# Attention with a threshold and a squared-ReLU FFN on one core: weight norms from TensorE products, low words to integers on GpSimd, other prices in the planner

## The chip, the cores and the metric

One Trainium2 chip, one core of it. The metric is the device time of one execution in microseconds (us), given as the median of several runs. Beside it stands one execution taken with the hardware profiler, from which all durations inside the kernel come. The five engines of the core run their own instruction lists in fixed order: TensorE (PE, with its weight loads listed as PEld), VectorE (DVE), ScalarE (ACT), GpSimd (POOL) and SyncE (SP), which here issues all transfers.

## The reference

Eight batches, eight heads, 576 positions, 64 columns per head. Scores under the row maximum by more than tau are dropped; the result goes through an FFN with 512 columns in and out and 2048 in the middle.

```python
scores = scale * np.matmul(q, k.transpose(0, 1, 3, 2))
thresh = np.max(scores, axis=-1, keepdims=True) - tau
scores = np.where(scores >= thresh, scores, -1000000000.0)
attn = np.exp(scores - np.max(scores, axis=-1, keepdims=True))
attn = attn / (np.sum(attn, axis=-1, keepdims=True) + 1e-09)
x = np.matmul(attn, v)            # heads side by side: 4608 x 512
h = x @ w_in                      # 512 x 2048
r = np.maximum(h, 0.0)
out = (s * (r * r) + b) @ w_out   # 2048 x 512
```

The two weight matrices come as 64-bit floats. The core sees each number as two 32-bit words, the low one first.

## The kernel before

**Attention.** A tile is 128 queries of one head against 576 keys. Batch 0 (the "plain" tiles, 36 of them) is worked in 32-bit floats, because it runs while the weights aren't ready: scores on TensorE (L457), row maximum on VectorE (L460), threshold on GpSimd (L462), exponential on ScalarE (L464), mask and row sum on VectorE (L466), sum on GpSimd (L469), reciprocal on VectorE (L471), normalising on GpSimd (L472), five transposes on TensorE (L480), copy out on ScalarE (L484), product with V on TensorE (L493) and its copy on ScalarE (L497). The tiles of the other seven batches work with pairs of 16-bit pieces (L514 to L532), and with_v multiplies two heads' finished tiles by V (L547), one group of 28 products for 256 or 320 columns.

**FFN.** A block is 256 rows. For each of 16 slices f of the middle dimension a step makes 12 products with the pieces of w_in (L756), ReLU, square and split (L760 to L765), and 6 products with the pieces of w_out (L771). L685 sums the rows of w_out for the constant b.

**Weights.** A slice f of w_in and one of w_out, 128 x 512 numbers each, are loaded by load_weights (L567, L570) from the SyncE queue, 512 KB apiece. In weights, ScalarE turns the high word so that it becomes, once shifted by three bits, the upper part of a 32-bit float (L589); VectorE shifts it (L592); ScalarE squares the high word alone (L594, L603), TensorE sums the squares of w_in over rows with a matrix of ones (L599), VectorE takes the maximum (L601), and the squares of w_out are summed by ScalarE itself. pieces_of_weights joins the low word's three highest bits to it (whole, L645). When all 32 norms are there, weight_scales finds powers of two for the two matrices (L610 to L627). Only with these can ScalarE and VectorE make the 16-bit pieces (L653, L658) that the FFN's products need.

**Order.** Every operation is given to a planner (class Plan) with its engine, the time that it occupies the engine, the time to its result, what it reads and writes, and a due time in tiles. The planner places all operations by these prices, forward and backward several times, and keeps the order with the earliest end. Operations of GpSimd, and those of VectorE that are marked dve2, exclude each other in the planner. The result is a fixed order for each engine. Prices thus don't only describe the work, they decide the order of everything. On SyncE the weight loads stand in one queue with the loads of q, k and v, later with the moves of attention pieces (L370, L537) and the stores.

At the start, 76 products on zeros (L901) keep TensorE occupied while nothing else is there.

Of the kernel before, what the change touches and what calls it, by code (L numbers as in the profile page):

```python
# [9 lines left out]
F32 = mybir.dt.float32  # L10
F32R = mybir.dt.float32r
F16, BF16 = mybir.dt.float16, mybir.dt.bfloat16
I32 = mybir.dt.int32
# [127 lines left out]
def tile_attention_ffn(ctx: ExitStack, tc: tile.TileContext, qT, kT, v, tau, w_in, w_out, s, b, out):  # L141


    nc = tc.nc
# [38 lines left out]
    wmost, wnorm, wpower, wback = const("wmost", [P, 2, NF]), const("wnorm", [P, 4]), const("wpower", [P, 4, 2]), const("wback", [P, 2])  # L183
    ones16, onesb = const("ones16", [P, P], F16), const("onesb", [P, P], BF16)
# [355 lines left out]
    def with_v(g, at):  # L540
# [8 lines left out]
        cost = len(slots) * (0.42 * g.n + 8) + 300  # L549
# [11 lines left out]
    def load_weights(f, at):  # L561
# [8 lines left out]
        plan.add("SP", (1800, 6700), lambda: nc.sync.dma_start(out=raw(1).rearrange("p f t -> p (f t)"),  # L570
                                           in_=w_out[f * P:(f + 1) * P, :]), [], [(f"w{f}", "o")], at)

    def weights(f, at):
# [6 lines left out]
        tag = f"t{f % 2}"  # L580

# [3 lines left out]
        def squares():  # L585
            return early("eb")[:, 2 * DM * (f % 2):2 * DM * (f % 2) + DM // 2].bitcast(BF16)
        for u, k in (0, "i"), (1, "o"):
            kr = f"w{f}", k
            act((563, 667), lambda u=u: nc.scalar.activation(  # L589
                out=words(1, u).bitcast(F32), in_=words(1, u).bitcast(F32), func=AF.Prelu, scale=2.0 ** -112, alpha=-2.0 ** 32),  # L590
                [kr], [kr], at)
            dve2((328, 418), lambda u=u: nc.vector.tensor_scalar(  # L592
                out=words(1, u), in0=words(1, u), scalar1=3, scalar2=None, op0=ALU.logical_shift_left), [kr], [kr], at)
        act((563, 667), lambda: nc.scalar.activation(out=squares(), in_=words(1, 0).bitcast(F32), func=AF.Square),  # L594
            [(f"w{f}", "i")], [tag], at)

        def sizes():
            for c in range(NC):
                nc.tensor.matmul(bank["h"][:, 0:P], onesb, squares()[:, c * P:(c + 1) * P], start=(c == 0), stop=(c == NC - 1))  # L599
        pe(NC, P, sizes, [tag, "ones16"], ["h"], at)  # L600
        dve((200, 290), lambda: nc.vector.tensor_reduce(  # L601
            out=wmost[:, 0, f:f + 1], in_=bank["h"][:, 0:P], axis=mybir.AxisListType.X, op=ALU.max), ["h"], [("wmost", 0, f)], at)
        act((640, 860), lambda: nc.scalar.activation(  # L603
            out=early("eb")[:, 2 * DM * (f % 2) + DM // 2:2 * DM * (f % 2) + DM].bitcast(BF16), in_=words(1, 1).bitcast(F32),
            func=AF.Square, accum_out=wmost[:, 1, f:f + 1]), [(f"w{f}", "o")], [("wmost", 1, f), (tag, 1)], at)

    def weight_scales(at):

        most = [("wmost", u, f) for u in range(2) for f in range(NF)]
        dve((90, 170), lambda: nc.vector.tensor_reduce(  # L610
            out=wnorm[:, 0:2], in_=wmost, axis=mybir.AxisListType.X, op=ALU.max), most, ["wnorm"], at)
        dve((90, 170), lambda: nc.vector.tensor_reduce(
            out=wnorm[:, 2:3], in_=wmost[:, 1], axis=mybir.AxisListType.X, op=ALU.add), most, [("wnorm", 2)], at)
        top = bank["pv"][:, 384:386]
        pe(1, 64, lambda: nc.tensor.matmul(top, ones.bitcast(F32), wnorm[:, 2:4], start=True, stop=True),
           ["ones", "wnorm", ("wnorm", 2)], [("top", 384)], at)
        dve((72, 155), lambda: nc.vector.tensor_scalar(
            out=wpower[:, 0, 0:1], in0=wnorm[:, 0:1], scalar1=LEAST, scalar2=None, op0=ALU.max), ["wnorm"], ["wpower"], at)
        dve((72, 155), lambda: nc.vector.tensor_scalar(
            out=wpower[:, 0, 1:2], in0=top[:, 0:1], scalar1=LEAST, scalar2=None, op0=ALU.max), [("top", 384)], ["wpower"], at)  # L620
# [19 lines left out]
    def pieces_of_weights(f, at):  # L640

        def whole(u):
            raw = lazy["raw", f, u]
# [382 lines left out]
```

## Time and profile before

| | us |
|---|---|
| median of 3 runs | 1164.04 (1164.00 to 1165.47) |
| profiled execution, its own time | 1164.36 |
| profiled execution, span from the first to the last instruction | 1162.6 |
| TensorE busy | 1126.4 |
| ScalarE busy | 930.3 |
| VectorE busy | 858.7 |
| GpSimd busy | 779.2 |
| mean granted TensorE clock | 0.997 of full |

Busy times count an instruction from its first to its last moment. Neighbouring instructions of one engine overlap by a little, so what an instruction takes of its engine is the distance to the next one, or the piece that the chain of waits gives it, and it is shorter than the shown duration. Matmul ends are modelled. The idle time "before" a group is put down to what released it last.

### The profile page before, as it was taken

What the parts mean: (1) busy time and instruction counts of PE and PEld (TensorE: products, weight loads), DVE (VectorE), ACT (ScalarE), POOL (GpSimd) and SP (SyncE); (2) the same over time, 40 slices, a digit from 0 to 9 for tenths busy, and PEclk for the clock granted to TensorE, in tenths of its full rate; (3) what the DMA queues carried; (4) which work ended last, traced back from release to release, by engine and by line L of the source; (5) the groups of instructions that cost most, each with busy time, mean ns of one, the idle gap of its engine ahead of it and who ended that gap; (6) DMA issues with size and microseconds to landing.
All of it is one profiled execution on the core that took longest, in us unless ns stands there. A gap on an engine that the chain in (4) does not pass through costs nothing.

```text
span 1162.6 us, 26056 instructions
## 1 busy us (share of the span) xinstructions
PE 1126.4 (97%) x8778; PEld 820.4 (71%) x8778; DVE 858.7 (74%) x1840; ACT 930.3 (80%) x2159; POOL 779.2 (67%) x1327
## 2 busy tenths in 40 slices
PE   8888999989999999999999999999999999999998
PEld 7666766657777777766777777777777777766665
DVE  7998898897887888897778877788787878730011
ACT  4999898878889898987888888878888889754443
POOL 4568688777877787776667777778777878532200
PEclk9999999989999999999999999999999999999999
DMA  7930278998799788987778878887878779800000
GB/s 246 392 106 22 52 140 166 177 182 174 149 173 178 156 160 173 165 169 141 156 136 161 152 154 151 163 151 149 173 155 166 138 146 185 123 19 1 19 19 19
DMA packets 361334, 164.52 MB, mean 142 GB/s; under 512 B 315120, under 2 KB 336112, under 8 KB 361200
## 3 DMA queue, kind: packets, MB, share of 16 engines
q1 hardware_dynamic: 361200, 162.86, 68.7%
q8 instruction: 69, 1.13, 0.4%
q14 instruction: 65, 0.53, 0.1%
HBM read 62.52 MB, written 9.44 MB: 62 GB/s over the span
## 4 chain that ended last, share of the span: by engine, by line
PE 78%; ACT 7%; DVE 5%; DMA 5%; issue 2%; POOL 2%; SPq 2%; DVEq 0%; ACTq 0%; POOLq 0%
PE h L756 29%; PE o L771 29%; PE pv L547 8%; PE s L514 5%; PE t L514 5%; DMA iw<-in_moe_w_in_dram 2%; DMA eb<-en 1%; ACT en L529 1%; ACT em L521 1%; DVE st L517 1%; DVE en L532 1%; DVE em L523 1%; ACT em L464 1%; DVE iw L785 1%; ACT iw L760 1%
## 5 line engine op out<-in xcount | busy, mean ns | idle before, releaser
L756 PE MATMUL h<-xp,iw 128*128 128x256 f16 x3456 | 427.1, 273 | 7.3 <-ACT iw L760 5.5
L756 PEld LDWEIGHTS <-iw 128*128 128x128 f16 x3456 | 330.1, 98 | 91.5 <-issue 11.3
L771 PE MATMUL o<-ow,gh 128*128 128x512 f16 x1080 | 322.9, 381 | 1.0 <-DVE iw L785 1.0
L765 POOL TENSOR_TENSOR gl<-iw,gh 128x256 f16<-128x256 f32 x272 | 199.8, 735 | 125.1 <-ACT gh L764 95.8
L532 DVE SCALAR_TENSOR_TENSOR en<-em,st,en 128x576 f16<-128x576 f32 x252 | 237.2, 947 | 23.8 <-ACT en L529 22.8
L529 ACT ACTIVATE en<-em,st 128x576 f16<-128x576 f32 x252 | 192.9, 771 | 19.3 <-DVE st L528 14.7
L771 PE MATMUL o<-ow,gl 128*128 128x512 f16 x540 | 204.8, 379 | 0.0
L760 ACT ACTIVATE iw<-h 128x256 f32<-128x256 f32 x288 | 109.6, 380 | 118.9 <-PE h L756 112.3
L771 PEld LDWEIGHTS <-gh 128*128 128x128 f16 x1152 | 100.3, 98 | 78.0 <-issue 5.1
L519 POOL TENSOR_SCALAR st<-st,bound 128x1 f32<-128x1 f32 x252 | 108.4, 431 | 52.4 <-DVE st L517 27.7
L763 ACT ACTIVATE iw<-iw 128x256 f32<-128x256 f32 x288 | 120.0, 417 | 3.8
L764 ACT CAST gh<-iw 128x256 f16<-128x256 f32 x288 | 116.1, 404 | 5.4 <-PE o L771 1.0
L523 DVE SCALAR_TENSOR_TENSOR em<-s,st,em 128x576 f32<-128x576 f32 x126 | 102.3, 812 | 19.8 <-ACT em L521 10.4
L517 DVE TENSOR_REDUCE st<-t 128x1 f32<-128x576 f32 x126 | 94.9, 753 | 29.1 <-PE t L514 28.5
L526 POOL TENSOR_SCALAR st<-st 128x1 f32<-128x1 f32 x252 | 80.2, 318 | 53.1 <-DVE em L523 20.5
L523 DVE SCALAR_TENSOR_TENSOR em<-t,st,em 128x576 f32<-128x576 f32 x126 | 102.3, 812 | 18.1 <-ACT em L521 10.6
L517 DVE TENSOR_REDUCE st<-s 128x1 f32<-128x576 f32 x126 | 94.8, 753 | 27.7 <-PE s L514 26.2
L521 ACT ACTIVATE em<-t,st 128x576 f32<-128x576 f32 x126 | 92.7, 735 | 21.2 <-DVE st L517 16.0
L547 PE MATMUL pv<-ea,v 128*64 128x256 f16 (+1 forms) x784 | 107.9, 289 | 0.0
L547 PE MATMUL pv<-eb,v 128*64 128x256 f16 (+1 forms) x784 | 106.9, 288 | 0.5 <-DMA eb<-en 0.4
L521 ACT ACTIVATE em<-s,st 128x576 f32<-128x576 f32 x126 | 92.7, 736 | 16.0 <-DVE st L517 15.7
L771 PEld LDWEIGHTS <-gl 128*128 128x128 f16 x576 | 56.3, 98 | 67.9
(190 smaller groups left out, 1864.0 us busy)
## 6 DMA issues: line engine op xcount, KB each, us to landing
rk<-in_k_dram SPq DMA_DIRECT2D x57, 288.0 KB, 4.2
rq<-in_q_dram SPq DMA_DIRECT2D x56, 288.0 KB, 4.1
ow<-k SPq DMA_DIRECT2D x56, 216.0 KB, 2.9
iw<-in_moe_w_in_dram SPq DMA_DIRECT2D x16, 512.0 KB, 7.3
ow<-in_moe_w_out_dram SPq DMA_DIRECT2D x16, 512.0 KB, 7.9
out_dram<-iw SPq DMA_DIRECT2D x32, 256.0 KB, 3.0
rv<-in_v_dram SPq DMA_DIRECT2D x56, 128.0 KB, 2.8
kt<-k SPq DMA_DIRECT2D x56, 72.0 KB, 2.6
```

The source lines that it names most:

```text
L514: nc.tensor.matmul(ps[:, hf], stat, kk(hf), start=(n == 0), stop=(n == len(seq) - 1))
L517: dve((667, 750), lambda: nc.vector.tensor_reduce(out=top, in_=ps, axis=mybir.AxisListType.XY, op=ALU.max, negate=True), [bk], [(ks_, 0)], ...
L521: act((636, 740), lambda: nc.scalar.activation(out=halves, in_=ps, func=AF.Exp, bias=top, scale=1.0), [bk, (ks_, 0)], [em_k], i - 0.5)
L523: dve((740, 900), lambda: nc.vector.scalar_tensor_tensor(out=halves, in0=ps, scalar=line, in1=halves, op0=ALU.is_ge, op1=ALU.mult, accum_o ...
L529: act((668, 774), lambda: nc.scalar.activation(out=pieces[:, 0:S], in_=ex, func=AF.Copy, scale=unit), [em_k, (ks_, 3)], [en_k], i)
L532: dve2((740, 825), lambda: nc.vector.scalar_tensor_tensor(out=pieces[:, S + T:2 * S + T], in0=ex, scalar=unit, in1=pieces[:, 0:S], op0=ALU ...
L547: nc.tensor.matmul(ps[j * D:(j + 1) * D], hd.v[:, (n + 1) % 5, u * D:(u + 1) * D], lazy[("ea", "eb")[j]][:, n, g.c0:g.c0 + g.n], start=(i ...
L756: nc.tensor.matmul(ps, wi[w][f][:, c * P:(c + 1) * P], x[:, u, c, :], start=(c == 0 and i == 0), stop=(c == NC - 1 and i == 2))
L760: act((357, 473), lambda: nc.scalar.activation(out=g(), in_=ps, func=AF.Relu, scale=H_DOWN), [h, (f"w{(0, 1, 5)[k3]}", "i", 2)], [kg], at)
L763: act((320, 417), lambda: nc.scalar.activation(out=g(), in_=g(), func=AF.Square), [kg], [kg], at)
L765: do((712, 735) if not self.last else (340, 425), lambda: eng.tensor_tensor(out=lo, in0=g(), in1=hi, op=ALU.subtract), [kg, f"gh{k3}"], [f ...
L771: nc.tensor.matmul(bank["o"][:, t, :], a[:, ts_], w, start=(f == 0 and i == 0), stop=(f == NF - 1 and i == 2))
```

## The change

- **Squares and shifts go.** L592, L594, L599, L601 and L603 with their scratch space are removed. ScalarE's only work per weight piece before the scales is L589.
- **Low words on GpSimd.** A new instruction per piece (32 in all) reads the upper 16 bits of each low word as an unsigned 16-bit integer (one of four half words, a step of 8 bytes), multiplies by 2^-13 and subtracts just under one half, and writes the result as a 32-bit integer over the low word: its three highest bits.
- **The join shifts.** whole now shifts the high word left by three and joins the new integer, in one VectorE instruction as before. It stands in weights, ahead of the norms, and has to wait for GpSimd.
- **Norms from products.** A new function weight_sizes, once for four slices, reads the upper halves of the joined floats as 16-bit floats (bf16, every second half word) and lets TensorE multiply each 128 x 128 part with itself: 16 products for w_in into four stretches of 128 columns of a PSUM bank, VectorE's maximum over 512 columns, then 16 for w_out into 128 columns, and the maximum over these. No ones matrix in bf16 is made any more.
- **Scales.** weight_scales takes the maximum over four values for each matrix, turns the two columns through TensorE, takes the maximum over 128, multiplies by a 2 x 2 identity and spreads the two numbers over all partitions with one product. Before it had two reductions and one product.
- **Prices.** A group with V costs 14 (0.417 n + 3) + 150 ns in the plan for 14 (0.42 n + 8) + 300, and a weight load 1320 ns of the queue and 5200 ns to landing for 1800 and 6700.

```diff
-        cost = len(slots) * (0.42 * g.n + 8) + 300
+        cost = len(slots) * (0.417 * g.n + 3) + 150
...
-        plan.add("SP", (1800, 6700), lambda: nc.sync.dma_start(out=raw(0).rearrange("p (c f) t -> p c (f t)", c=NC),
+        plan.add("SP", (1320, 5200), lambda: nc.sync.dma_start(out=raw(0).rearrange("p (c f) t -> p c (f t)", c=NC),
...
+        def whole(u):
+            raw = lazy["raw", f, u]
+            lazy["whole", f, u] = raw.rearrange("p f t -> p (f t)")[:, 0:DM].bitcast(F32)
+            nc.vector.scalar_tensor_tensor(out=lazy["whole", f, u].bitcast(I32), in0=raw[:, :, 1], scalar=3, in1=raw[:, :, 0],
+                                           op0=ALU.logical_shift_left, op1=ALU.bitwise_or)
...
-            dve2((328, 418), lambda u=u: nc.vector.tensor_scalar(
-                out=words(1, u), in0=words(1, u), scalar1=3, scalar2=None, op0=ALU.logical_shift_left), [kr], [kr], at)
-        act((563, 667), lambda: nc.scalar.activation(out=squares(), in_=words(1, 0).bitcast(F32), func=AF.Square),
-            [(f"w{f}", "i")], [tag], at)
...
-        act((640, 860), lambda: nc.scalar.activation(
-            out=early("eb")[:, 2 * DM * (f % 2) + DM // 2:2 * DM * (f % 2) + DM].bitcast(BF16), in_=words(1, 1).bitcast(F32),
-            func=AF.Square, accum_out=wmost[:, 1, f:f + 1]), [(f"w{f}", "o")], [("wmost", 1, f), (tag, 1)], at)
+            pool((700, 720), lambda u=u: nc.gpsimd.tensor_scalar(
+                out=words(0, u), in0=lazy["raw", f, u].bitcast(U16)[:, :, 1], scalar1=2.0 ** -13, scalar2=2.0 ** -14 - 0.5,
+                op0=ALU.mult, op1=ALU.add), [kr], [kr + (0,)], at)
+            dve2((602, 685), lambda u=u: whole(u), [kr, kr + (0,)], [kr], at)
+
+    def weight_sizes(k, at):
+        fs, d = range(4 * k, 4 * k + 4), [slice(c * P, (c + 1) * P) for c in range(NC)]
+
+        def top(f, u):
+            return lazy["whole", f, u].bitcast(BF16).rearrange("p (f t) -> p f t", t=2)[:, :, 1]
+
+        def grams(u):
+            for n, f in enumerate(fs):
+                for c in range(NC):
+                    nc.tensor.matmul(bank["h"][:, d[0 if u else n]], top(f, u)[:, d[c]], top(f, u)[:, d[c]],
+                                     start=(c == 0 and not (u and n)), stop=(c == NC - 1 and (not u or n == 3)))
+        for u, key, w in (0, "i", 4 * P), (1, "o", P):
+            pe(4 * NC, P, lambda u=u: grams(u), [(f"w{f}", key) for f in fs], ["h"], at)
+            dve((100 + 1.06 * w, 190 + 1.06 * w), lambda u=u, w=w: nc.vector.tensor_reduce(
+                out=wmost[:, u, k:k + 1], in_=bank["h"][:, 0:w], axis=mybir.AxisListType.X, op=ALU.max), ["h"], [("wmost", u, k)], at)
...
+        turned, top = bank["h"][0:2, 0:P], bank["pv"][:, 384:386]
+        pe(1, 4 * P, lambda: nc.tensor.matmul(turned, wnorm[:, 0:2], ident(), start=True, stop=True), ["ident", "wnorm"], ["h"], at)
+        dve((210, 290), lambda: nc.vector.tensor_reduce(
+            out=wnorm[0:2, 2:3], in_=turned, axis=mybir.AxisListType.X, op=ALU.max), ["h"], [("wnorm", 2)], at)
...
-            dve2((602, 685), lambda u=u: whole(u), [kr], [kr], at)
...
+        if f % 4 == 3:
+            events.append((WEIGHTS_EACH * f + 0.1, lambda f=f: weight_sizes(f // 4, 2.5 + WEIGHTS_EACH * f)))
```

More of the change, by code (lines that the diff above doesn't have):

```diff
@@ L12 @@
 F16, BF16 = mybir.dt.float16, mybir.dt.bfloat16
-I32 = mybir.dt.int32
+I32, U16 = mybir.dt.int32, mybir.dt.uint16
 AF = mybir.ActivationFunctionType
@@ L182, in tile_attention_ffn @@
     power = [const(f"power{i}", [P, 5, 4]) for i in range(2)]
-    wmost, wnorm, wpower, wback = const("wmost", [P, 2, NF]), const("wnorm", [P, 4]), const("wpower", [P, 4, 2]), const("wback", [P, 2])
-    ones16, onesb = const("ones16", [P, P], F16), const("onesb", [P, P], BF16)
+    wmost, wnorm, wpower, wback = const("wmost", [P, 2, 4]), const("wnorm", [P, 4]), const("wpower", [P, 4, 2]), const("wback", [P, 2])
+    wtop = const("wtop", [P, 2])
+    ones16 = const("ones16", [P, P], F16)
     vs = [const(f"vs{i}", [P, 4]) for i in range(2)]
@@ L607, in weight_scales @@
     def weight_scales(at):
-        most = [("wmost", u, f) for u in range(2) for f in range(NF)]
+        most = [("wmost", u, k) for u in range(2) for k in range(4)]
         dve((90, 170), lambda: nc.vector.tensor_reduce(
             out=wnorm[:, 0:2], in_=wmost, axis=mybir.AxisListType.X, op=ALU.max), most, ["wnorm"], at)
-        dve((90, 170), lambda: nc.vector.tensor_reduce(
-            out=wnorm[:, 2:3], in_=wmost[:, 1], axis=mybir.AxisListType.X, op=ALU.add), most, [("wnorm", 2)], at)
@@ L617, in weight_scales @@
         dve((72, 155), lambda: nc.vector.tensor_scalar(
-            out=wpower[:, 0, 0:1], in0=wnorm[:, 0:1], scalar1=LEAST, scalar2=None, op0=ALU.max), ["wnorm"], ["wpower"], at)
+            out=wtop[0:2], in0=ident()[0:2, 0:2], scalar1=wnorm[0:2, 2:3], scalar2=None, op0=ALU.mult), [("wnorm", 2), "ident"], ["wtop"], at)
+        pe(1, 64, lambda: nc.tensor.matmul(top, ones.bitcast(F32), wtop, start=True, stop=True), ["ones", "wtop"], [("top", 384)], at)
         dve((72, 155), lambda: nc.vector.tensor_scalar(
-            out=wpower[:, 0, 1:2], in0=top[:, 0:1], scalar1=LEAST, scalar2=None, op0=ALU.max), [("top", 384)], ["wpower"], at)
+            out=wpower[:, 0], in0=top, scalar1=LEAST, scalar2=None, op0=ALU.max), [("top", 384)], ["wpower"], at)
@@ L640, in pieces_of_weights @@
     def pieces_of_weights(f, at):
-        def whole(u):
-            raw = lazy["raw", f, u]
-            lazy["whole", f, u] = raw.rearrange("p f t -> p (f t)")[:, 0:DM].bitcast(F32)
-            nc.vector.scalar_tensor_tensor(out=lazy["whole", f, u].bitcast(I32), in0=raw[:, :, 0], scalar=29, in1=raw[:, :, 1],
-                                           op0=ALU.logical_shift_right, op1=ALU.bitwise_or)
         def high(u):
@@ L894, in zeros @@
         nc.gpsimd.memset(ones16, 1.0)
-        nc.gpsimd.memset(onesb, 1.0)
     pool((700, 700), zeros, [], ["ones", "qt0", "qt1", "ones16"], -10)
@@ L911, in bounds @@
     def bounds():
-        for t in [vm.bitcast(F32), wnorm] + norm:
+        for t in [vm.bitcast(F32), wtop] + norm:
             nc.gpsimd.memset(t, 0.0)
-    pool((900, 900), bounds, [], ["vm", "norm0", "norm1", "wnorm", ("wnorm", 2)], -8)
+    pool((900, 900), bounds, [], ["vm", "norm0", "norm1", "wtop"], -8)
     def margins():
```

14 lines of the change are left out of this document (1 added, 13 removed).

## The prediction

> **What bounds the kernel now.** I read the page first, then stretches of the early part, then groups and the chain in the stretch that the change touches. TensorE looks saturated in the mean:
>
> ```profile
> span 1162.6 us, 26056 instructions
> PE 1126.4 (97%) x8778; PEld 820.4 (71%) x8778; DVE 858.7 (74%) x1840; ACT 930.3 (80%) x2159; POOL 779.2 (67%) x1327
> ```
>
> The mean hides two stages. The windows (columns: window, its length, then the busy time of each engine with its count, granted clock, DMA share, GB/s) part them:
>
> ```profile
> 30.00:60.00 30.00, 25.65 (x226) 20.41 (x225) 29.39 (x73) 29.55 (x61) 16.41 (x30) 1.00 1.06 394
> 23.00:90.00 67.00, 58.45 (x519) 45.89 (x520) 64.48 (x163) 65.79 (x134) 39.82 (x72) 1.00 0.71 251
> 90.00:98.00 8.00, 6.48 (x47) 4.71 (x45) 7.73 (x20) 5.40 (x13) 7.38 (x12) 1.00 0.00 1
> ```
>
> And two rows with the times of the stage: L589 rewrites weights from 23.1 us on, and the first conversion with the scales, L653, starts at 97.7 us.
>
> ```profile
> L589 ACT ACTIVATE iw<-iw x16: 667/705/777, 23.1 to 83.0; 128x512 f32<-128x512 f32 x16
> ```
> ```profile
> 97.70 1.34 ACT iw L653 x2
> ```
>
> From 23 us to 90 us, within which all squares are taken (the groups below count 16 and 16 of them), ScalarE is busy 65.8 of 67 us and VectorE 64.5: both are full, while TensorE works on tiles of batch 0 only (its busy time includes the modelled tails of matmuls, so it has more air than it shows). The weight scales come out at 97.7 us, and only then can the big products of L756 and L771 start. After that TensorE has more work than it can do: what it waits for from 110 us to the end is small, the largest two being
>
> ```profile
> PE h L756 <- ACT iw L760: 5.0, 7, 1.0
> PE t L514 <- DVE em L523: 4.1, 4, 2.4
> ```
>
> (total us, times, longest). So the end moves with the time at which TensorE gets weights, less what it does of batch 0 meanwhile. The change works exactly on the 23 to 98 us stage, and, by the plan's prices, on the order of everything.
>
> **ScalarE: the squares go.** Groups between 23 and 90 us, then pieces of the chain, which give what one instruction takes of its engine:
>
> ```profile
> L589 ACT ACTIVATE ow<-ow 128x512 f32<-128x512 f32 x16 | 11.5, 719 | 0.0
> L589 ACT ACTIVATE iw<-iw 128x512 f32<-128x512 f32 x16 | 11.4, 712 | 0.0
> L603 ACT ACTIVATE eb<-ow 128x512 bf16<-128x512 f32 x16 | 11.4, 721 | 0.0
> L594 ACT ACTIVATE eb<-iw 128x512 bf16<-128x512 f32 x16 | 11.2, 702 | 0.0
> ```
> ```profile
> 47.68 0.58 ACT eb L594
> 49.45 0.67 ACT eb L603 x2
> ```
>
> 16 x 0.58 + 16 x 0.67 = 20.0 us of ScalarE go. In the stage it falls from 65.8 to about 46 of 67 us: it stops being a bound.
>
> **VectorE: shifts and small maxima go, joins come forward.**
>
> ```profile
> L645 DVE SCALAR_TENSOR_TENSOR iw<-iw 128x512 int32<-128x512 int32 x13 | 8.9, 685 | 0.1
> L645 DVE SCALAR_TENSOR_TENSOR ow<-ow 128x512 int32<-128x512 int32 x13 | 8.9, 682 | 0.0
> L592 DVE TENSOR_SCALAR iw<-iw 128x512 int32<-128x512 int32 x16 | 7.1, 444 | 0.1
> L592 DVE TENSOR_SCALAR ow<-ow 128x512 int32<-128x512 int32 x16 | 6.9, 431 | 0.3 <-ACT ow L589 0.2
> L601 DVE TENSOR_REDUCE wmost<-h 128x1 f32<-128x128 f32 x16 | 4.5, 280 | 0.2
> ```
> ```profile
> 65.75 0.34 DVE iw L592
> 66.21 0.20 DVE wmost L601
> 94.94 0.75 DVE wpower L621
> 95.69 0.60 DVE iw L645
> 96.36 0.59 DVE ow L645
> ...
> 249.55 0.67 DVE st L517
> ```
>
> Removed: 32 x 0.34 + 16 x 0.20 = 14.1 us. Added: four maxima over 512 columns and four over 128. The latter are 0.20 each; the former lie between that 0.20 for 128 columns and the 0.67 that a maximum over 576 columns takes (L517), and I take 0.67: 4 x 0.87 = 3.5 us. Moved: the join (L645 before) must now stand ahead of the products, and 6 of the 32 joins are today done after 90 us; they come into the stage, 6 x 0.60 = 3.6 us. VectorE goes from 64.5 to about 57.5 of 67 us. It too stops being the bound.
>
> **GpSimd: 32 new instructions.** Nothing before shows 16-bit integers turned into 32-bit ones on GpSimd. Nearest is its scaling of 512 floats, L324; the low bound is that row, the high one the mean with waits of L472 in this stage (0.82):
>
> ```profile
> L324 POOL TENSOR_SCALAR k<-k,bound x2: 686/688/691, 15.6 to 80.5; 128x512 f32<-128x512 f32 x2
> L472 POOL TENSOR_SCALAR em<-em,st x36: 737/746/1750, 12.2 to 135.2; 128x576 f32<-128x576 f32 x36
> L462 POOL TENSOR_SCALAR st<-st,bound x36: 260/448/1217, 9.5 to 130.4; 128x1 f32<-128x1 f32 x36
> L469 POOL TENSOR_SCALAR st<-st x36: 190/258/761, 11.2 to 133.7; 128x1 f32<-128x1 f32 x36
> ```
> ```profile
> L472 POOL TENSOR_SCALAR em<-em,st 128x576 f32<-128x576 f32 x21 | 17.1, 817 | 10.6 <-DVE st L471 6.9 <-PE h L599 1.5 <-DVE norm L722 1.4
> L462 POOL TENSOR_SCALAR st<-st,bound 128x1 f32<-128x1 f32 x20 | 10.6, 532 | 8.1 <-DVE st L460 7.9
> L469 POOL TENSOR_SCALAR st<-st 128x1 f32<-128x1 f32 x20 | 5.9, 296 | 8.2 <-DVE em L466 7.3
> ```
>
> (First fence: shortest/median/longest of the whole run in ns.) I take 0.69, so 32 x 0.69 = 22.1 us. Looked at alone GpSimd has room: 39.8 + 22.1 = 62 of 67. But look at how a one-column instruction that takes 0.26 can take 0.62:
>
> ```profile
> 50.83 0.68 DVE L645 SCALAR_TENSOR_TENSOR ow<-ow 128x512 int32<-128x512 int32 x1
> 51.02 0.62 POOL L462 TENSOR_SCALAR st<-st,bound 128x1 f32<-128x1 f32 x1 [0.72 <-DVE st L460]
> ```
>
> It began inside a join and ended 0.13 us after it: the two engines exclude each other while VectorE reads two tensors. So the joins, the shifts and all of GpSimd share one resource. Its demand in the stage before: 21 x 0.74 + 20 x 0.26 + 20 x 0.19 = 24.5, plus GpSimd's other 11 instructions as shown (39.8 - 17.1 - 10.6 - 5.9 = 6.2), plus 26 x 0.60 + 32 x 0.34 = 26.5: 57.2 of 67 us. After: -10.9 for the shifts, +3.6 for the six joins, +22.1: 72.0 of 67. A bound at 98% has been swapped for one at 107%. What eases it is the 0.13 just seen: an instruction of 0.26 had done half of its work under the wait. If half of GpSimd's then 104 instructions win 0.13 each, the demand is 65.2. So the stage ends between 1.8 us sooner and 5 us later; I take **+1.0**, nearer the easy end because the waiting pair is seen in the trace.
>
> The Trainium skill, page SBUF — State Buffer, section "Who interferes with whom", states the rule for this: a VectorE instruction with two SBUF inputs contends with a GpSimd instruction that reads SBUF, and the one that comes second is fully blocked. By that rule taken strictly nothing overlaps and the stage is 5 us longer, not 1; the trace agrees on the blocking (0.62 for 0.26), not on the whole duration. The Trainium skill's page GPSIMD Engine Reference, section "7. Performance pitfalls for Q7 kernels", puts about 1.9 cycles on an element at strides up to 8 bytes, which the new instruction just keeps; at the 1.2 GHz of its section "1. Specifications" an estimate by that page of the skill is 0.81 us in place of 0.69, or 3.8 us more on the shared resource. No row here has a strided GpSimd read.
>
> **TensorE** gets 128 products of 128 columns for 64, some 4 us more over 67 us, in which it waits for batch 0's tiles; they cost nothing while it waits, 4 us if it were full.
>
> **The way from the last weight to the scales.** Today: square, sum, maximum, scales. After: integers (0.69), join (0.60), 16 + 16 products (about 1 us each) with a maximum behind each group, then a turn through TensorE, one more maximum, one more multiplication. Over the shift (0.34) and square (0.67) this is 0.69 + 0.60 + 1.0 + 0.2 - 1.0 = 1.5, and the turn with its maximum, multiplication and hand-overs some 1.8: 3.3 us later. TensorE goes on with tiles meanwhile; I charge half, **+1.6** (bounds 0 and 3.3). Against it, the joins leave the stretch behind 90 us: two lie on the chain itself (95.69 and 96.36 above), 1.2 us, and four more held up VectorE before the first weights; half of their 2.4 counts: **-2.4** together (bounds -3.6 and -1.2).
>
> **Tiles run smoother.** TensorE's waits for ScalarE between 8 and 98 us,
>
> ```profile
> PE pv L493 <- ACT rv L484: 3.1, 3, 1.3
> PE t L480 <- ACT x L484: 2.8, 3, 1.1
> ```
>
> stood behind squares in ScalarE's queue. With 20 us of air a part goes, though each tile now passes a fuller GpSimd three times: **-1.6** (bounds -5.9 and +3).
>
> **The plan's prices.** A group of products with V is priced 14 x (0.42 n + 8) + 300: 1.92 us for 256 columns and 2.29 for 320; the new price gives 1.69 and 2.06. The trace has
>
> ```profile
> 294.29 2.02 PE pv L547 x28
> 311.77 1.65 PE pv L547 x28
> ```
>
> so the new price is right, and 56 groups no longer pretend 15 us of TensorE time. This alters the order on every engine until 1020 us. What a truer order can win is bounded by TensorE's waits there (9.1 us in the two largest rows); it can lose as easily. **-2.0** (bounds -6 and +4). A weight load is priced 1.32 us of the queue for 1.8; 512 KB at the 394 GB/s above is 1.33, so this is right too. Its landing is priced 5.2 us for 6.7, while the page has
>
> ```profile
> iw<-in_moe_w_in_dram SPq DMA_DIRECT2D x16, 512.0 KB, 7.3
> ```
>
> and that is too early by 2.1; the list of waits up to 100 us names no weight load, so it costs nothing as long as the engines run behind the loads, and 2.1 once if they don't.
>
> **The sum**, against the profiled execution (1164.36 us, of which 1162.6 is the span; the median of the runs is 1164.04, 0.3 less): +1.0 + 1.6 - 2.4 - 1.6 - 2.0 = -3.4, so **1161 us**. Its own bounds, with the terms not all at one end: 1154 to 1168.
>
> **Rivals.**
> *VectorE sets the stage.* If the overlap of GpSimd and the joins is larger than seen, the stage shrinks towards VectorE's 57.5 us. Half of the 9.5 us gained reaches the end, since fewer tiles are then done at that time: 1161 - 5 - 3 (the plan's term at its good end) = 1153. For it: VectorE and ScalarE are the engines that show full. Against: the 0.62.
> *The shared port decides* (the slower side). Every join and every GpSimd instruction excludes the other in full: 72.0 for 67, +5.0, with the longer way to the scales in full, +3.3, and only the two joins on the chain saved, -1.2: 1164.4 + 7.1 = 1171. It decides from the point at which the demand passes 67 us: with no overlap, a new instruction of 0.53 us; with half overlapped, one of 0.75. The strict rule of the Trainium skill's page SBUF — State Buffer, cited above, is this rival.
> *The loads are expected too early.* With the landing priced 2.1 us short, ScalarE and VectorE stop in their fixed order on weights between 23 and 60 us, and input loads of batch 0 on the same SyncE queue fall behind weights while DMA is at 1.06 of its share: 2.1 for the first weight, about as much for one late tile: 1168.
> *Nothing moves.* One full resource takes the place of another, and the new order wins nothing: 1164.
>
> **Chances.** Forecast 0.42, of which 0.06 ends within 0.2% (2.3 us, about what a measurement of this kernel can tell from no change); VectorE sets the stage 0.11; nothing moves 0.15; shared port 0.25; early loads 0.07. So faster 0.36 + 0.11 = 0.47, within 0.21, slower 0.32. The range for 8 in 10 reaches to the VectorE case on one side and to the port case on the other: 1152 to 1172; the forecast's own is 1154 to 1168.
>
> **What would show it.** The stage: between the first and the last join, VectorE under 90% and ScalarE near 70% if the shared resource is the bound; GpSimd's new instruction 0.69 alone and stretched beside joins; joins of 0.68 growing to 1 us and more. The first L653 after 97.7 us means the stage didn't shorten; before 93 the VectorE rival. The plan: TensorE's waits behind 110 us. The forecast is wrong if the scales come over 4 us later or earlier than today, or if the difference arises after 150 us.

## The result: 1175.9 us, slower by 0.9%

| | before | after |
|---|---|---|
| median of four runs each, us | 1164.4 (1164.0 to 1165.5) | 1175.9 (1174.7 to 1177.2) |
| profiled execution, us | 1164.36 | 1177.11 |
| its span, us | 1162.6 | 1175.3 |
| mean granted TensorE clock | 0.997 | 0.991 |

The ratio is 1.0088 with a 95% interval [1.0072, 1.0104] (the two medians alone stand as 1.0099). The forecast of 1161 us was wrong, and so was its range up to 1172. The page's first lines after:

```profile
span 1175.3 us, 26160 instructions
PE 1136.5 (97%) x8844; PEld 830.2 (71%) x8844; DVE 853.7 (73%) x1800; ACT 911.7 (78%) x2111; POOL 803.1 (68%) x1358
```

ScalarE gave up 18.6 us, VectorE 5.0, GpSimd took 23.9 more, and TensorE started 66 more products. The windows of the changed kernel (columns as in the prediction):

```profile
23.00:90.00 67.00, 58.17 (x524) 46.17 (x523) 55.72 (x121) 46.15 (x81) 58.88 (x93) 0.97 0.68 224
30.00:45.00 15.00, 10.98 (x92) 8.79 (x92) 10.80 (x23) 9.11 (x16) 13.69 (x20) 0.89 0.93 314
90.00:98.00 8.00, 7.53 (x82) 6.16 (x81) 7.40 (x14) 4.51 (x8) 7.48 (x13) 1.00 0.60 147
180.00:220.00 40.00, 33.58 (x238) 24.06 (x236) 34.26 (x71) 30.16 (x69) 27.30 (x49) 0.91 0.94 180
260.00:280.00 20.00, 14.13 (x94) 9.36 (x91) 17.89 (x38) 13.73 (x28) 14.47 (x26) 0.83 0.96 177
```

TensorE starts 524 products from 23 to 90 us for 519, although 112 of them serve the norms for 64 before: tiles fell back. In the same window ScalarE is at 46.2 us (the prediction had about 46) and VectorE at 55.7 (57.5). GpSimd is busy 58.9 of 67 us, and 13.7 of 15 between 30 and 45 us, a stretch in which every other engine has air. But two later stretches stand out as much: TensorE is busy 33.6 of 40 us at 180 and 14.1 of 20 at 260, at a clock of 0.91 and 0.83. Before, the same stretches read

```profile
180.00:220.00 40.00, 37.47 (x301) 27.21 (x299) 32.52 (x71) 34.77 (x84) 32.96 (x53) 1.00 0.85 165
260.00:280.00 20.00, 20.00 (x166) 14.83 (x166) 15.68 (x37) 17.06 (x43) 14.86 (x23) 0.95 0.88 182
```

**A ledger of TensorE.** Busy time is a poor measure of a pipelined engine. So I count the products in stretches of 8 to 100 us and give each a price, most of them from undisturbed pieces of the chain: 0.1105 us for one of L759 (1.33 for 12), 0.2165 for L774 (0.65 for 3), 0.0655 for L548 (the mean of 1.65 and 2.02 for 28), 0.1235 for L515 (the chain has 0.52 for 4, so 0.13, a little more), 0.2425 for L458 (0.97 for 4), 0.11 for L481 (0.55 for 5), 0.062 for L494, 0.217 for L688, and about 0.06 for a product that serves the norms. What is left of the time is "idle" (waits, products on zeros, and what a halved clock costs). A product that lies across the border of two stretches counts in both, so idle time is understated, and not by the same amount in every run; a difference of 1 or 2 us in it means nothing. Counted once, by its start, the first row of the table is 34.4 and 36.4, the second 18.7 and 27.7, the third 24.3 and 22.5.

| idle, us | before | after |
|---|---|---|
| from 0 to 110 us | 33.1 | 33.7 |
| from 110 to 300 us | 15.5 | 24.6 |
| from 300 to 1100 us | 20.5 | 18.9 |

The span grew by 12.7 us. Some 4 of these are, by count and price, the 64 additional products, and idle time up to 110 us did not shrink to make up for them. Another 9.1 come between 110 and 300 us, long after the changed stage; 1.6 come back later. The prediction had named this as a sign against it: a difference that arises after 150 us.

**What the stage looks like.** Timeline rows of the changed kernel, first VectorE, then GpSimd, then ScalarE (start, us, engine, line; in brackets the idle time before and what ended it):

```profile
31.62 0.70 DVE L587 SCALAR_TENSOR_TENSOR ow<-ow 128x512 int32<-128x512 int32 x1 [0.65 <-POOL ow L595]
32.88 0.69 DVE L587 SCALAR_TENSOR_TENSOR iw<-iw 128x512 int32<-128x512 int32 x1 [0.55 <-POOL iw L595]
...
36.40 0.69 DVE L587 SCALAR_TENSOR_TENSOR iw<-iw 128x512 int32<-128x512 int32 x1 [1.32 <-POOL iw L595]
```
```profile
30.92 0.67 POOL L595 TENSOR_SCALAR ow<-ow 128x512 int32<-128x512 uint16 x1
31.67 1.17 POOL L595 TENSOR_SCALAR iw<-iw 128x512 int32<-128x512 uint16 x1
```
```profile
42.64 0.69 ACT L485 COPY rv<-t 128x640 f32<-128x640 f32 x1 [4.60 <-PE t L481]
```

A new integer instruction (L595) takes 0.64 to 0.67 us alone. The next one begins 0.05 us after a join and lasts 1.17: it ends 0.52 us after the join, so of its 0.65 only 0.13 went on under the join, the very overlap that the prediction read from the 0.62 of L462. The rule of the Trainium skill, page SBUF — State Buffer, section "Who interferes with whom", is that the ports which the two share are an exclusive lock; that is nearly what the trace shows. The next join waits for this integer, and a little later ScalarE waits 4.60 us for transposes: between 30.9 and 37.6 us GpSimd runs five integers among its work for the tiles. Where the chain of waits before was ScalarE's from 43 to 64 us, with squares in it, GpSimd's work stands in it after, from 65 to 74 us:

```profile
65.75 1.19 POOL iw L595
67.02 0.70 POOL st L470
...
68.82 0.72 POOL em L473
...
69.87 0.66 POOL ow L595
```

Between 23 and 90 us the joins wait 6.0 us for integers:

```profile
L587 DVE SCALAR_TENSOR_TENSOR iw<-iw 128x512 int32<-128x512 int32 x16 | 12.7, 797 | 3.3 <-POOL iw L595 3.3
L595 POOL TENSOR_SCALAR iw<-iw 128x512 int32<-128x512 uint16 x16 | 12.3, 771 | 1.3
L595 POOL TENSOR_SCALAR ow<-ow 128x512 int32<-128x512 uint16 x15 | 11.4, 760 | 1.2
...
L587 DVE SCALAR_TENSOR_TENSOR ow<-ow 128x512 int32<-128x512 int32 x14 | 10.4, 743 | 2.7 <-POOL ow L595 2.7
```

The first conversion starts at 107.9 us, 10.2 later than before, the last product for the norms at 96.0:

```profile
L610 PE MATMUL h<-ow x64: 218/218/221, 43.4 to 96.0; 128*128 128x128 bf16 x64
```
```profile
L657 ACT ACTIVATE iw<-iw,wpower x16: 705/711/739, 107.9 to 145.9; 128x512 f16<-128x512 f32 x16
```

**What a late stall looks like.** Rows of TensorE and of GpSimd at 196 us, then the transfer as a piece of the chain:

```profile
194.58 1.47 PE L759 MATMUL h<-xp,iw 128*128 128x256 f16 x12
195.81 0.77 PE L515 MATMUL s<-k,qs 128*128 128x288 f32 x4
199.84 2.72 PE L759 MATMUL h<-xp,iw 128*128 128x256 f16 x12 [3.27 <-ACT iw L763]
```
```profile
195.86 0.74 POOL L374 TENSOR_SCALAR rq<-rq,bound 128x576 f32<-128x576 f32 x1 [2.55 <-DMA rq<-in_q_dram]
```
```profile
191.38 4.31 DMA rq<-in_q_dram
```

A load of queries takes 4.31 us from its issue, GpSimd stands 2.55 us before it with its work for V (L419) queued behind, ScalarE's ReLU (L763) stands in order behind the copy of that V, and TensorE waits 3.27 us. Then the 12 products take 2.72 us; the same 12 took 1.47 at 194.58 us. No weight load is involved; these come from the next batches' attention.

### The profile page after: what moved, and what is told of

Its sections match the earlier page's. It is cut to its first block, busy times and chain, and to the rows that moved or that the text cites. A ratio compares the mean times of both kernels' runs of the same rounds, so it can differ in the third digit from the quotient of the medians.

```text
span 1175.3 us, 26160 instructions
## 1 busy us (share of the span) xinstructions
PE 1136.5 (97%) x8844; PEld 830.2 (71%) x8844; DVE 853.7 (73%) x1800; ACT 911.7 (78%) x2111; POOL 803.1 (68%) x1358
## 4 chain that ended last, share of the span: by engine, by line
PE 78%; DMA 7%; ACT 4%; DVE 4%; issue 2%; POOL 2%; SPq 2%; DVEq 0%; ACTq 0%; POOLq 0%
PE h L759 30%; PE o L774 29%; PE pv L548 7%; PE t L515 5%; PE s L515 5%; DMA ow<-in_moe_w_out_dram 2%; DMA rq<-in_q_dram 1%; DMA iw<-in_moe_w_in_dram 1%; ACT en L530 1%; DVE em L524 1%; ACT em L522 1%; DMA k<-in_q_dram 1%; PE pv L494 1%; DMA ea<-en 1%; DVE iw L788 1%
## 5 line engine op out<-in xcount | busy, mean ns | idle before, releaser
L759 PE MATMUL h<-xp,iw 128*128 128x256 f16 x3456 | 429.4, 274 | 6.4 <-ACT iw L763 5.8
L759 PEld LDWEIGHTS <-iw 128*128 128x128 f16 x3456 | 330.7, 98 | 91.7 <-issue 12.7
L774 PE MATMUL o<-ow,gh 128*128 128x512 f16 x1080 | 323.4, 381 | 2.7 <-DVE iw L788 2.7
L774 PE MATMUL o<-ow,gl 128*128 128x512 f16 x540 | 204.9, 379 | 1.3 <-POOL gl L768 1.3
L763 ACT ACTIVATE iw<-h 128x256 f32<-128x256 f32 x288 | 109.4, 380 | 120.5 <-PE h L759 111.4
L520 POOL TENSOR_SCALAR st<-st,bound 128x1 f32<-128x1 f32 x252 | 115.4, 458 | 64.2 <-DVE st L518 31.0
L774 PEld LDWEIGHTS <-gh 128*128 128x128 f16 x1152 | 101.9, 99 | 76.2 <-issue 7.3
L524 DVE SCALAR_TENSOR_TENSOR em<-s,st,em 128x576 f32<-128x576 f32 x126 | 102.2, 811 | 19.8 <-ACT em L522 10.8
L527 POOL TENSOR_SCALAR st<-st 128x1 f32<-128x1 f32 x252 | 80.0, 318 | 50.4 <-DVE em L524 22.5
L518 DVE TENSOR_REDUCE st<-s 128x1 f32<-128x576 f32 x126 | 94.8, 752 | 27.1 <-PE s L515 25.9
L522 ACT ACTIVATE em<-t,st 128x576 f32<-128x576 f32 x126 | 92.8, 736 | 20.5 <-DVE st L518 17.5
L548 PE MATMUL pv<-ea,v 128*64 128x256 f16 (+1 forms) x784 | 107.5, 288 | 0.0
L548 PE MATMUL pv<-eb,v 128*64 128x256 f16 (+1 forms) x784 | 107.0, 288 | 0.3 <-DMA eb<-en 0.2
L774 PEld LDWEIGHTS <-gl 128*128 128x128 f16 x576 | 56.4, 98 | 70.2 <-POOL gl L768 2.3
```

Of the source, the lines that this page charges most:

```text
L518: dve((667, 750), lambda: nc.vector.tensor_reduce(out=top, in_=ps, axis=mybir.AxisListType.XY, op=ALU.max, negate=True), [bk], [(ks_, 0)], ...
L522: act((636, 740), lambda: nc.scalar.activation(out=halves, in_=ps, func=AF.Exp, bias=top, scale=1.0), [bk, (ks_, 0)], [em_k], i - 0.5)
L524: dve((740, 900), lambda: nc.vector.scalar_tensor_tensor(out=halves, in0=ps, scalar=line, in1=halves, op0=ALU.is_ge, op1=ALU.mult, accum_o ...
L548: nc.tensor.matmul(ps[j * D:(j + 1) * D], hd.v[:, (n + 1) % 5, u * D:(u + 1) * D], lazy[("ea", "eb")[j]][:, n, g.c0:g.c0 + g.n], start=(i ...
L759: nc.tensor.matmul(ps, wi[w][f][:, c * P:(c + 1) * P], x[:, u, c, :], start=(c == 0 and i == 0), stop=(c == NC - 1 and i == 2))
L774: nc.tensor.matmul(bank["o"][:, t, :], a[:, ts_], w, start=(f == 0 and i == 0), stop=(f == NF - 1 and i == 2))
```

## The experiments

There were two theories at the start: **the shared port** (the integers on GpSimd exclude VectorE's joins and delay the tiles) and **the order** (the planner, given other operations and prices, found a worse order, which has little to do with what the engines can do). Ratios are against the kernel before on the same chip.

**Prices alone, weights alone.** The kernel before with the three new prices, and the changed kernel with the three old ones.

```diff
-        cost = len(slots) * (0.42 * g.n + 8) + 300
+        cost = len(slots) * (0.417 * g.n + 3) + 150
-        plan.add("SP", (1800, 6700), ...
+        plan.add("SP", (1320, 5200), ...
```

> The kernel before with only the three new prices of the plan (group with V, weight load). If the prices made the loss that arises behind 180 us, about 8 of the 12 us: 1172. If the weights' new work made all of it: 1164, within 2.

> The kernel after with the old prices. If the weights' work makes the loss: 1176. If the prices make the part behind 180 us: 1168, of which 4 are the 64 additional products on TensorE.

Prices alone: 1163.4, ratio 0.9988 [0.9977, 1.0000]. Weights alone: 1170.2, 1.0041 [1.0023, 1.0060]. The second lies between its two expectations. The loss sits with the weights, as far as two orders can tell; the two parts, -2.1 and +4.7 us, don't add up to the 11.5 of the whole.

**Norms from products without the integers.** VectorE shifts and joins as before, everything else as after.

```diff
-            pool((700, 720), lambda u=u: nc.gpsimd.tensor_scalar(
-                out=words(0, u), in0=lazy["raw", f, u].bitcast(U16)[:, :, 1], ...), [kr], [kr + (0,)], at)
+            dve2((328, 418), lambda u=u: nc.vector.tensor_scalar(
+                out=words(1, u), in0=words(1, u), scalar1=3, scalar2=None, op0=ALU.logical_shift_left), [kr], [kr + (0,)], at)
...
-  in0=raw[:, :, 1], scalar=3, in1=raw[:, :, 0], op0=ALU.logical_shift_left, ...
+  in0=raw[:, :, 0], scalar=29, in1=raw[:, :, 1], op0=ALU.logical_shift_right, ...
```

> The kernel after, with VectorE shifting the high word as before and joining the unchanged low word; GpSimd gets no integers to make, the norms stay products. If GpSimd and the access that it shares with VectorE set the stage: scales near 97 us instead of 107.7, and 1168 or less. If VectorE (10.9 us fuller) or the longer way to the scales does: scales beyond 104 us and 1174 or more.

1159.4, ratio 0.9952 [0.9932, 0.9971]: faster than both kernels. Its stage:

```profile
23.00:90.00 67.00, 62.16 (x585) 50.05 (x585) 64.56 (x154) 49.41 (x88) 47.07 (x82) 1.00 0.71 228
```

TensorE starts 585 products here for 524 of the changed kernel, 116 of them for the norms for 112, with VectorE at 64.6 us and GpSimd at 47.1. The scales were expected near 97 us and the first conversion starts at 100.6, later than the 97.7 before: the moment of the first conversion doesn't tell what the stage gained.

**The integers on ScalarE.** A copy with scale and bias in place of GpSimd's instruction.

```diff
-            pool((700, 720), lambda u=u: nc.gpsimd.tensor_scalar(
+            act((563, 667), lambda u=u: nc.scalar.activation(
```

> The kernel after with the 32 integer instructions on ScalarE, which has some 20 us of air, at about 0.58 us each. If GpSimd sets the stage: scales near 95 us, 1166 or less. If it was the order or the products: no better than 1174.

1162.0, 0.9971 [0.9956, 0.9987], and the smallest idle time up to 110 us of all, 23.7. ScalarE is busy 64.5 of 67 us there, nearly what it was before, with VectorE at 58.9:

```profile
23.00:90.00 67.00, 61.97 (x591) 49.53 (x590) 58.85 (x129) 64.53 (x119) 46.50 (x81) 1.00 0.74 233
```

So a full ScalarE is no harm by itself. Before, VectorE was full as well (64.5 us); that the two together made the difference fits, but no run tests it. Nor does this run part the two ways in which integers on GpSimd can hurt: GpSimd's fixed queue with more work in it, and its exclusion by the joins.

**The integers with the old squares.** New prices, integers and shifting join, but norms from ScalarE's squares of the joined floats and the ones matrix.

```diff
+            pool((700, 720), lambda u=u: nc.gpsimd.tensor_scalar(out=words(0, u), ...
+            dve2((602, 685), lambda u=u: whole(u), [kr, kr + (0,)], [kr], at)
-            dve2((328, 418), lambda u=u: nc.vector.tensor_scalar( ... scalar1=3 ...
```

> The new prices with GpSimd's integers and the shifting join ahead of the norms, but ScalarE's squares (of the joined floats) and the ones products kept: the GpSimd part alone. Theory 'GpSimd and its shared access are the price': 1163 for the prices alone plus what the integers cost under the new norms (1176 - 1159 = 16), so 1176 to 1182, since ScalarE has less air here. Theory 'it needs the products too': 1166 to 1170.

1170.1, 1.0036 [1.0016, 1.0056]. Against the prices alone (1163.4) this order loses 6.7 us, far less than the 13 to 19 that were expected if the integers alone were the price, and near the other expectation, that the loss needs the products too.

**One nanosecond.** To see how much is order, the price of a group with V is made 1 ns larger, in the changed kernel and in the one without integers.

```diff
-        cost = len(slots) * (0.417 * g.n + 3) + 150
+        cost = len(slots) * (0.417 * g.n + 3) + 151
```

> The kernel after with the price of a group with V one ns higher (0.05%), which means nothing but may turn the order. If the loss behind 180 us is a matter of this one order: anywhere between 1166 and 1178. If it belongs to the change: 1174 to 1178.

> The version without GpSimd's integers (VectorE shifts and joins, norms from products), with the same nudge of one ns. If that version's 1159 is of the order's luck: up to 1168. If it is of the work: 1157 to 1162.

1179.1 for 1175.9 (two runs, 1.0119 [1.0069, 1.0169]), and 1165.3 for 1159.4 (0.9998 [0.9987, 1.0009]). A nanosecond that describes no work moves the second by 6 us, clear of its interval; the 3 us of the first lie within it.

**The changed kernel's order with GpSimd left empty.** The plan is made as if the integers were there; GpSimd's place stays empty and VectorE shifts directly ahead of each join.

```diff
-            pool((700, 720), lambda u=u: nc.gpsimd.tensor_scalar( ... ), [kr], [kr + (0,)], at)
+            pool((700, 720), lambda: None, [kr], [kr + (0,)], at)
...
+            nc.vector.tensor_scalar(out=words(1, u), in0=words(1, u), scalar1=3, scalar2=None, op0=ALU.logical_shift_left)
```

> The order of the kernel after on every engine, with nothing in GpSimd's 32 places and the shift set directly ahead of each join on VectorE (0.94 us in place of 0.60). If GpSimd's occupied time and its shared access make the loss: scales at 101 us or earlier and 1162 to 1167. If it is the order that the plan made for it: 1172 or more.

1178.5, 1.0114 [1.0080, 1.0148], though GpSimd is at 34.0 us:

```profile
23.00:90.00 67.00, 54.97 (x502) 43.45 (x502) 64.64 (x140) 42.72 (x76) 33.96 (x58) 0.97 0.67 223
```

I first took this for proof of the order theory. It isn't one: 22 us were taken off GpSimd, but 32 x 0.34 = 11 us that the plan didn't know of went to VectorE, which is at 64.6 us with only 502 products started. For the stage it shows that GpSimd's being occupied isn't needed for such a loss, no more. For the late loss it shows more. TensorE and ScalarE work off the same instructions in the same order as in the changed kernel, and the two late stretches come out the same:

```profile
180.00:220.00 40.00, 33.90 (x236) 23.91 (x235) 33.54 (x70) 30.26 (x68) 28.04 (x50) 0.91 0.97 175
260.00:280.00 20.00, 14.59 (x97) 9.86 (x97) 17.76 (x39) 14.10 (x31) 14.37 (x27) 0.83 0.92 178
```

So the late loss goes with this order and doesn't need the integers. (The first conversion is as late, at 109.6 us, so a part of the late start in it isn't excluded.)

**The integers unpriced.** The reverse: they run, but the plan takes them for nearly nothing.

```diff
-            pool((700, 720), lambda u=u: nc.gpsimd.tensor_scalar(
+            pool((20, 720), lambda u=u: nc.gpsimd.tensor_scalar(
```

> The changed kernel with one price altered: the planner believes that an integer instruction takes GpSimd for 20 ns instead of 700, so it orders the other work almost as if the 32 were not there, while the chip still runs them. If the order made around them is the cause, the time falls to that of the kernel without them: 1158 to 1166. If the time that they really take of GpSimd and of the shared port is the cause, the late work piles up unforeseen and it stays at 1172 to 1180. If both take part, between: 1167 to 1171.

1174.5, 1.0092 [1.0062, 1.0121]. Idle time up to 110 us is 33.8, as in the changed kernel (33.7). An order that makes no room for them doesn't avoid the loss.

**Integers for half of the pieces.** GpSimd for w_out alone.

```diff
+            if u:
                 pool((700, 720), lambda u=u: nc.gpsimd.tensor_scalar( ...
+            else:
+                dve2((328, 418), lambda u=u: nc.vector.tensor_scalar( ...
```

> The changed kernel with GpSimd's integers for the 16 pieces of w_out alone; the 16 of w_in keep the shift and the old join. If the loss goes by the time on GpSimd, half of it: 1166 to 1169. If it begins only where the shared port is over-full, the demand here is 72.0 - 11.0 + 5.4 = 66.4 of 67 us, just under: 1159 to 1164. If the order is luck alone, anywhere between 1159 and 1176.

1167.9, 1.0021 [1.0003, 1.0039], with 25.8 us idle up to 110 us, no more than without any. In this one order the stage loses nothing by 16 integers, and 6 us by 32 in the mean of four, as a resource does that is just not full and then over-full. The whole, at 1167.9, fits the other expectation, half the loss, so the time alone doesn't decide between the two.

**Products with the old prices, and the kernel before nudged.**

```diff
-        cost = len(slots) * (0.42 * g.n + 8) + 300
+        cost = len(slots) * (0.42 * g.n + 8) + 301
```

> Norms from products with VectorE's shift and the old join, no integers on GpSimd, and the old three prices. With the new prices this gave 1159.4, and 1165.3 after a nudge of one price. If the products themselves gain some 4 us, 1159 to 1163 here too. If the 1159.4 was luck of the order, 1164 to 1168.

> The kernel before with a single price made 1 ns larger (the group with V, 301 for 300), which says nothing about any work. If the order alone moves the time by several us, this differs from the kernel before by 3 to 6 us to one side, as the two other nudges did (+3 and +6). If the kernel before is a settled order, it stays within 2 us of it.

1177.8 for the products with old prices, 1.0119 [1.0085, 1.0154], 18 us more than with the new ones and outside both expectations, though its idle time up to 110 us is the same (27.7 for 27.5); some 7 us more are idle between 110 and 300 us and some 10 from 300 to 1100. And the kernel before takes 1169.2 with one nanosecond more, 1.0039 [1.0008, 1.0071]. With this, single comparisons of two orders were worth little, and the last six runs went into samples: three designs, four orders each, told apart by this price alone.

In the kernel before 299 and 302 for 300, in the two others 152 and 153 for 150, as in

```diff
-        cost = len(slots) * (0.417 * g.n + 3) + 150
+        cost = len(slots) * (0.417 * g.n + 3) + 152
```

> The kernel before, the price of a group with V 1 ns smaller (299). If the design sets the time: 1163 to 1168. If the order does: anywhere from 1159 to 1176. TensorE's idle time until 110 us stays at 33 to 36 us either way, if that stage is the design's.

> The changed kernel, the same price 3 ns larger (153). If the design sets the time: 1174 to 1180. If the order does: anywhere from 1162 to 1180. Idle until 110 us 33 to 36 us if the early stage is the design's.

> Products without integers on GpSimd (1159.4 and, nudged by 1 ns, 1165.3), the same price 3 ns larger. If the design sets the time: 1159 to 1166. If the order does: anywhere up to 1178. Idle until 110 us 27 to 28 us if the early stage is the design's.

> The kernel before, the price of a group with V 2 ns larger (302). Design: 1163 to 1170. Order: anywhere from 1159 to 1176. Idle until 110 us 33 to 36 us.

> The changed kernel, the same price 2 ns larger (152). Design: 1174 to 1180. Order: anywhere from 1162 to 1180. Idle until 110 us 33 to 36 us.

> Products without integers on GpSimd, the same price 2 ns larger. Design: 1159 to 1166. Order: anywhere up to 1178. Idle until 110 us 27 to 28 us.

| design | added to the price, ns | us | ratio [95%] | idle 0-110 | 110-300 | 300-1100 |
|---|---|---|---|---|---|---|
| before | 0 | 1165.2 | 1 | 33.1 | 15.5 | 20.5 |
| | +1 | 1169.2 | 1.0039 [1.0008, 1.0071] | 36.4 | 18.6 | 19.2 |
| | -1 | 1168.4 | 1.0024 [1.0010, 1.0038] | 35.4 | 21.0 | 17.7 |
| | +2 | 1170.3 | 1.0041 [1.0025, 1.0057] | 36.9 | 19.1 | 22.5 |
| after | 0 | 1175.9 | 1.0088 [1.0072, 1.0104] | 33.7 | 24.6 | 18.9 |
| | +1 | 1179.1 | 1.0119 [1.0069, 1.0169] | 36.1 | 23.0 | 23.7 |
| | +2 | 1172.9 | 1.0070 [1.0048, 1.0093] | 34.0 | 19.2 | 20.9 |
| | +3 | 1164.8 | 0.9995 [0.9982, 1.0008] | 30.3 | 16.3 | 21.0 |
| after, without integers | 0 | 1159.4 | 0.9952 [0.9932, 0.9971] | 27.5 | 12.6 | 19.8 |
| | +1 | 1165.3 | 0.9998 [0.9987, 1.0009] | 27.3 | 18.6 | 20.7 |
| | +2 | 1169.6 | 1.0040 [1.0024, 1.0056] | 25.5 | 21.5 | 26.1 |
| | +3 | 1165.5 | 1.0012 [0.9994, 1.0029] | 27.8 | 14.5 | 23.6 |

(Each time is the median of its own runs, on several chips; each ratio is against the kernel before on the same chip.) Two things follow. In the early stage the design sets the number: 25.5 to 27.8 us without integers, 30.3 to 36.1 with them, 33.1 to 36.9 before; the first group touches neither of the others. Counted once, by start, the groups are 27.1 to 29.7, 32.3 to 38.2 and 34.4 to 38.1, and the same holds. Behind 110 us the order does: 12.6 to 24.6 us between 110 and 300, whatever the design. The changed kernel with 3 ns more is as fast as the kernel before, and of the four orders of the kernel before the one given is the fastest. Its stage with 3 ns more still has GpSimd at 59.7 us:

```profile
23.00:90.00 67.00, 59.70 (x550) 47.08 (x550) 57.38 (x123) 46.29 (x81) 59.65 (x96) 1.00 0.73 235
260.00:300.00 40.00, 39.00 (x327) 29.67 (x327) 34.09 (x74) 36.15 (x86) 31.32 (x54) 1.00 1.00 177
```

The means of the ratios are 1.0026 before, 1.0068 after and 1.0001 without integers. With the scatter inside each group (standard deviations 0.0019, 0.0053 and 0.0037), the change as a design costs 0.42% with a standard error of 0.28%, some 5 of the 11.5 us, and that is not settled; the integers cost 0.68% with 0.32%, about two standard errors with four orders each, so in the time they are likely and not certain, while the idle times of the stage part clearly. The version without them, in the order of its unaltered prices, is the fastest kernel run here; that its design is faster than the one before (0.26% with 0.21%) isn't shown.

## Why the prediction was wrong

The step that failed is the sum's term for the **order**. It was -2.0 with bounds -6 and +4, put down to the prices and bounded by TensorE's waits in the old order, and all other terms were taken as if the rest of the 1160 us stayed as it was. Between 110 and 300 us the given order loses **9.1 us** more than the one before, outside those bounds (7.5 with what comes back later), and the run with GpSimd left empty repeats this loss in the same order. One nanosecond alters the idle time of that stretch by 1.6 to 6.0 us (before 15.5 to 18.6 and 21.0, after 24.6 to 23.0, without integers 12.6 to 18.6), and 3 ns take it to 16.3 in the changed kernel, so this loss is no property of the operations that were changed. The uncertainty of the order belonged on the whole change.

Beside it, "they cost nothing while it waits" isn't borne out for this order. TensorE's 64 additional products take **some 4 us** by count and price, and idle time up to 110 us came out at 33.7 for 33.1, not 4 lower. In one place TensorE even stood 1.8 us before such a product, waiting for a join (the second row is its weight load, which waits at the same time):

```profile
PE h L610 <- DVE iw L587: 1.8, 1, 1.8
PEld L610 <- DVE iw L587: 2.0, 1, 2.0
```

How much of the 4 us filled waits can't be told, because the other terms move the same idle time; without integers it falls by more than 4.

The other terms, against idle time up to 110 us:

- *Shared port, +1.0 (bounds -1.8 and +5).* The size was off. With all integers the stage has 33.5 us idle in the mean of four orders, without them 27.0: **+6.5**, by the strict bound of +5 rather than by the middle. The overlap of 0.13 was right for a pair (0.13 again at 31.67 us), but I let half of GpSimd's instructions win it. That the exclusion is the whole of it isn't shown: it is seen beside joins, but GpSimd's longer queue alone could hold tiles up too, and no run parts the two. The integers' mean with waits was 0.77 and 0.76 us for the 0.69 charged. That it "decides from the point at which the demand passes 67 us" agrees with the one order with half of them: 72.0 - 11.0 + 5.4 = 66.4, and no loss.
- *Tiles run smoother, -1.6 (bounds -5.9 and +3).* Far too small. Without integers the idle time falls from 35.5 to 27.0 in the mean: **-8.5**, with whatever the other changes of that version do to it. I had bounded it by TensorE's waits for ScalarE alone. What the squares held up beyond these waits was not traced. ScalarE's load alone was not the point: with the integers on ScalarE it is as full as before and the stage has the least idle time of all.
- *A longer way to the scales, +1.6 (0 to 3.3).* From the last product for the norms to the first conversion it takes 107.9 - 96.0 = 11.9 us after. Before, by the row below, it is 97.7 - 87.1 = 10.6: **+1.3**. In the other three orders of the design after it is 7.9, 10.1 and 9.3, in those of the kernel before 10.3, 11.3 and 10.1, so no lengthening shows. The 1.8 us that the prediction put on the turn through TensorE and its hand-overs is worked out from no row. The rest of the 10.2 us by which the conversions came later lies ahead of it: the last product for the norms stands 8.9 us later.

```profile
L599 PE MATMUL h<-eb,onesb x64: 217/219/230, 26.8 to 87.1; 128*128 128x128 bf16 x64
```

- *Joins out of the stretch behind 90 us, -2.4.* Two of the 32 still stand there for 6 before (14 and 16 of them start ahead of 90 us, the last at 94.5), VectorE is busy 7.4 of its 8 us all the same, and the conversions came 10.2 us later. No gain can be told.
- *Plan's prices, -2.0.* Alone they gave 1163.4 for 1165.5, -2.1. It looks like a hit and isn't: the same kernel moves by 3 to 5 us with one or two nanoseconds.

So by this ledger the stage nets -8.5 + 6.5 + 4 = +2.0 us in the mean, where the prediction had -1.4. (With products counted once the two differences are -7.9 and +6.7.) What the given order loses beyond that is order. The rows named in the prediction were mostly as it said: VectorE under 90% (55.7 of 67), ScalarE near 70% (46.2), an integer 0.67 alone and up to 1.17 beside a join, the first conversion behind 97.7. Only joins of 1 us and more stayed out as a rule; the mean is 0.80 and 0.74.

Of the rivals, the shared port at 1171 came nearest in time, and its mechanism fits the stage, but isn't the cause of the whole 11.5 us: in this order the stage accounts for 4 to 6 of them, the additional products included. That 1171 lies nearest is luck. VectorE setting the stage and loads expected too early were not seen; the longest direct wait for a weight load in the stage is 0.2 us (TensorE, once), and the longest for an input load is 1.5 us in both kernels. What makes one order lose 12 us between 110 and 300 us and another 25 stays open in part. Up to 6.8 of these 12 us are the halved clock that follows waits (last section); what makes the waits was traced at one place. The stall at 196 us shows the kind: a load or a copy of the next batch stands ahead of the FFN's ReLU in one of the fixed queues.

## What to carry to other kernels

Where a planner fixes the order of thousands of instructions, one run of a change says little below the scatter of its orders, here 5 to 14 us for each design: alter a price that means nothing by a nanosecond or two, a few times on both sides, and compare groups. Read the changed stage by itself as well, by counted work and not by busy time, for there a design shows even when the end doesn't. And before work is moved to GpSimd to ease VectorE, add up what the two exclude each other for: half of the integers cost the stage nothing in the one order tried, all of them 6 us in the mean of four.

## What was unexpected in the hardware

A gap on TensorE can cost twice. After 3.27 us without a product, the next 12 took 2.72 us in place of 1.47, and the same is seen at 113.84 us, where the chain has

```profile
113.84 2.69 PE h L759 x12
116.53 1.42 PE s L458 x4
...
121.94 1.31 PE h L759 x12
```

although the gap ahead was only 1.10 us, with five transposes of 0.77 us and another gap of 0.81 before them. The windows (the third figure from the end is the granted clock) show a halved clock over both groups, and how busy TensorE was in the 3.41 us ahead:

```profile
110.48:113.90 3.42, 1.51 (x13) 1.02 (x11) 3.25 (x6) 3.42 (x8) 3.14 (x5) 1.00 0.00 0
113.90:117.31 3.41, 3.41 (x15) 2.46 (x15) 2.56 (x4) 2.62 (x7) 2.84 (x5) 0.50 0.00 0
195.82:199.23 3.41, 0.75 (x7) 0.62 (x5) 1.97 (x4) 2.21 (x5) 3.18 (x6) 1.00 1.00 269
199.23:202.65 3.42, 2.81 (x14) 2.14 (x14) 2.56 (x7) 3.35 (x9) 3.18 (x6) 0.50 0.61 143
```

In the changed kernel's trace the clock is halved five times after the start and before the end, from 38.81, 113.90, 199.23, 209.47 and 270.91 us, for 3.41 us each and 6.83 the last time; all lie whole multiples of 3.41 us apart. In the 3.41 us ahead of each, TensorE was busy for 0.40 to 1.51 us; of the other stretches on this beat from 20 to 1140 us none at full clock has under 2.2. Over all runs the halved clock follows 0 to 2.1 us, and from 1.5 us up some stretches went without it. The Trainium skill, page TensorE: Matmul & The Clock Gate, Part 1, tells of half the clock after one idle window of about 3.4 us that runs freely. The trace agrees on the length and on the fixed beat; but none of these five windows was empty.

A halved clock costs at most half of its length. Between 110 and 300 us that is 8.5 us after for 3.4 before (255.03 to 261.85), so up to 5.1 of the 9.1 us that the late stretch loses. Over the twelve orders, taking this half off turns the 12.6 to 24.6 us of that stretch into 10.9 to 17.9; the changed kernel with 3 ns more has no halved clock there, the one without integers in its given order 1.7 us of loss. By the granted clock (0.997 and 0.991 of the span) at most 0.006 x 1175 = 7 us of the whole difference are such slow stretches; they come with the waits and are contained in the idle time above.
